# Transposes by a 32-column selection matrix, and an expansion moved ahead of two stores, in a gated mix of attention and memory recurrence

## The chip, the cores and the metric

The kernel runs on one core of a Trainium2 chip. TensorE (PE) does the matrix products out of SBUF into PSUM, VectorE (DVE) and ScalarE (ACT) read PSUM and SBUF, GpSimd (POOL) works on SBUF alone, and SyncE (SP) and POOL issue the DMAs. Each engine takes its instructions in order, so an instruction that waits holds all that stand behind it on its engine. The metric is the device time of one execution in microseconds. Before the change its median is 6508.05 us, over 6 runs from 6499.43 to 6512.82.

## What is computed

Forward and backward of a gated mix of two branches over 2048 tokens of width 576. Branch A is attention with 32 query heads of 18 and one shared key and value head. Branch B is a recurrence over 64 segments of 32 tokens: 8 memory rows `mem` stand in front of the segment's tokens, attention with 32 heads of 128 runs over the 40 rows, and the memory's output rows are the next segment's memory.

```python
g = sigmoid((x * gate_w).sum(-1, keepdims=True))
a = A(x, A_wq, A_wk, A_wv, A_wo)
...
for s in range(n_seg):
    h = concatenate([mem, xs])
    q, k, v = h @ Wq, h @ Wk, h @ Wv        # 32 heads of 128
    p = softmax(where(mask, q @ k.T * scale, -1e9))
    o = (p @ v) @ Wo
    mem = o[:8]
    outs.append(o[8:])
return g * a + (1 - g) * b                   # and its gradients for 11 inputs
```

The loop over segments can't be run in parallel: segment s needs the memory that segment s − 1 leaves.

## The kernel before

**Two weaves.** `weave` (L211) runs two generators against each other. After each piece of the chain (up to its `yield`) it runs one step of the sweep. Within a weave the instructions stand on each engine in just this order; no scheduler moves them. In the forward weave (L1707) the chain is `b_chain_fwd`, which is the recurrence of B for the memory rows, and the sweep is `a_pass1`, the attention of A. In the backward weave (L1715) the chain is `b_chain_bwd` and the sweep is `a_pass2`.

**The sweep's step** is the same each time: two score products `a_S` (32 rows deep, 512 wide), two products `a_dP`, the exponential `a_E` of the scores on ACT (L1394), two products `a_W` on DVE (L1424) that read a_dP and a_E, and eight accumulation products `a_acc`. `a_S` has one buffer, so the scores of a step wait until the exponential of the step before has read it. `a_dP` has two, so each waits for the `a_W` that reads the step before. The backward sweep is built alike, with names b_S, b_dP, b_E (L1532), b_dS (L1553), b_acc. I call a piece of the chain with the step that follows it a slot. A segment has 16 pieces and a block of A's sweep has 16 steps, so the same pieces always meet: `a_post` (L1453) puts its transposes into the slots of k's and q's transposes, and its chain of small POOL operations, which ends with the product `a_qt` (L1494), in front of POOL's work on v.

**A segment of the forward chain.** The 8 memory rows (with 24 token rows that ride along) lie transposed in `hm`. For w in k, q, v two products of 512 columns by `proj` give row tiles `c_k2`, `c_q2`, `c_v2` of 128 partitions × 8 × 128 (the profile calls them c_k, c_q, c_v): partition 32c + r holds row r of head group c, and only r below 8 are memory rows. `mem_T` (L231) transposes such a tile: eight 128x128 transposes (L71) into one PSUM bank in bf16, of whose 128 columns per block 32 are read, the 8 memory rows of each of 4 groups. ACT copies k's and v's into `mT` (L308), and DVE copies q's into `c_qT` (L334). The row tiles go to DRAM by `rows_out` (L298, POOL's queue), and from there by `rows_copy` (L303 and L305, SP's queue) into the token tables. Then come scores, their exponential `c_E`, the denominators, and the probabilities `c_pn` (L366, DVE). `expand` (L205, POOL) spreads them over block diagonals `c_PB`. The pieces from v's second half on are these:

- v's second projection; the load of the next keys `c_kx` (SP); the store of v's rows `vrow_dram`; `c_pn`; its store `pm_dram` (L367); `c_PB`
- `rows_copy("q")` on SP; `mem_T` of v; its copy and store
- 16 products of `c_vx` and `c_v2` with `c_PB` into a tile `c_x`; DVE copies it to `c_oT` (L381)
- four pieces with the output projection (`half`, tile `c_pj`, copied by ACT to `c_hs`) and the sums that give the next segment's `hm`

**Backward.** In `b_chain_bwd` `mem_T` is called once per segment, on `dOm` (L856), and ACT copies the result to `r_dOT` (L858). `seln` (L136) is a constant selection matrix in bf16, 128 × (4 × 8), with a one where row 32c + q meets column (c, q). The backward chain already multiplies other row tiles by it (`r_x<-seln,r_dx`).

Of the kernel before, what the change touches and what calls it, by code (L numbers as in the profile page):

```python
# [9 lines left out]
BF16 = mybir.dt.bfloat16  # L10
F32 = mybir.dt.float32
P = 128
# [18 lines left out]
class Kern:  # L31
# [197 lines left out]
        return pj  # L229

    def mem_T(self, t2, psum, tag, bufs):  # L231
        pt = psum.tile([P, 8, P], BF16, name=tag, bufs=bufs)
        for u in range(8):
            self.tr(pt[:, u, :], t2[:, u, :], P)
        return pt[:].rearrange("p u (c t) -> p u c t", t=32)[:, :, :, 0:8]

    def b_chain_fwd(self, keep, sp, psum):
        nc = self.nc
# [21 lines left out]
        def load_k(s):  # L260
            kx = sp.tile([P, HB, 32], BF16, name="c_kx", bufs=1)
            nc.sync.dma_start_transpose(kx[:], self.xtok["k"][s * 32:(s + 1) * 32, :])
            return kx
# [23 lines left out]
        for s in range(NSEG):  # L287
            h_ = hm[s % 2]
            nc.gpsimd.dma_start(self.memT_dram[:, :, s, :], h_[:, :, 0:8])
            t2 = {w: sp.tile([P, 8, E], BF16, name=f"c_{w}2", bufs=1) for w in ("k", "q", "v")}  # L290
# [6 lines left out]
            def rows_out(w):  # L297
                nc.gpsimd.dma_start(self.row_dram[w][s], t2[w][:].rearrange("p u e -> p (u e)"))  # L298

            def rows_copy(w):  # L300
                src = self.row_dram[w][s].rearrange("(c r) e -> c r e", r=32)
                t0, n = ride(s)
                nc.sync.dma_start(self.mtok[w][s * 8:(s + 1) * 8, :].rearrange("r (c e) -> c r e", c=4), src[:, 0:8, :])  # L303
                if n:
                    nc.sync.dma_start(self.xtok[w][t0:t0 + n, :].rearrange("r (c e) -> c r e", c=4), src[:, 8:8 + n, :])  # L305
# [42 lines left out]
            for u in range(8):  # L348
                for c in range(4):
                    self.mm(ps[32 * c:32 * c + 8, 64 + 8 * u:72 + 8 * u], lhsT=mT["k"][:, c, u, :],  # L350
                            rhs=qT[:, u, c, :], start=False, stop=True, tp=(0, 32 * c))
# [9 lines left out]
            proj("v", 1)  # L361
            if s + 1 < NSEG:
                kx = load_k(s + 1)
            rows_out("v")
            pn = sp.tile([P, 2, 64], BF16, name="c_pn", bufs=1)
            nc.vector.tensor_tensor(out=pn[:], in0=Et[:], in1=rd[:].unsqueeze(1).to_broadcast([P, 2, 64]), op=ALU.mult)  # L366
            nc.gpsimd.dma_start(self.pm_dram[s], pn[:].rearrange("p a b -> p (a b)"))  # L367
            PB = sp.tile([P, 16, 4, 8], BF16, name="c_PB", bufs=1)
            self.expand(PB[:], pn[:].rearrange("p a (u q) -> p (a u) q", q=8), 16)
            yield  # L370
            rows_copy("q")
            src = self.mem_T(t2["v"], psum, "c_pj", 1)
# [1426 lines left out]
```

## Time and profile before

| | us |
|---|---|
| median of 6 runs | 6508.05 |
| the profiled execution, its own time | 6504.03 |
| its span, first to last instruction | 6501.8 |
| forward weave, about | 497 to 2470 |
| backward weave, about | 3285 to 5070 |

| in the trace | count | ns of one |
|---|---|---|
| transposes c_x<-identB,c_k and c_q; c_pj<-identB,c_v; r_x<-identB,r_dOm | 512 each | 219 |
| products c_x<-c_PB,c_vx; r_x<-seln,r_dx | 512 each | 176 |
| c_PB, POOL | 64 | 1084 |
| issue of vrow_dram, POOL | 64 | 607 |
| issue of pm_dram, POOL | 64 | 538 |
| c_qT from PSUM in bf16, DVE | 64 | 292 |
| c_oT from PSUM in F32, DVE | 64 | 425 |

A row of the timeline gives the start in us, the length in us, the engine, the line, the operation with output<-inputs, shapes and count, and in brackets how long the engine had been idle before it and what ended that. PEld is the loading of weights, which runs beside PE. Matmuls overlap: 8 of 219 ns take 0.61 us together. A wait's row gives the waiting operation and what it waited for, the total in us, how often, and the longest.

### The profile page before, as it was taken

The page shows a single profiled execution, that of the slowest core. Times are in us where ns is not written, and L with a number is a line of the kernel's source. Part 1 is how long each engine was busy: PE and PEld are TensorE (multiplying, and loading weights), DVE is VectorE, ACT ScalarE, POOL GpSimd, SP SyncE. Part 2 cuts the span into 40 slices and gives each one's busy share as a digit, 9 for nine tenths or more (in the row PEclk, how much of TensorE's full clock was granted, in tenths as well). Part 3 has the DMA queues.
Part 4 walks back from the last instruction along what each step waited for, and adds up shares of the span by engine and source line. Part 5 has one row for each costly group of instructions (what it writes and reads, how often), then busy time and mean ns, then how long its engine had stood idle before and what let it go on. Part 6 is the DMA issues. An engine that isn't in the chain of part 4 may idle for free. (4 is left out here: it accounts for less than half of the span.)

```text
span 6501.8 us, 208836 instructions
## 1 busy us (share of the span) xinstructions
PE 5984.0 (92%) x88822; PEld 3370.7 (52%) x88822; DVE 3770.0 (58%) x7061; ACT 3493.2 (54%) x5105; POOL 1960.4 (30%) x3451
## 2 busy tenths in 40 slices
PE   7898999999999995999969999999999899899997
PEld 5443444444444443877734444444444677675443
DVE  4336777777777773666658888888888211111111
ACT  3326777777777773666547777777777322211101
POOL 3002333333333333444423333333333111112212
PEclk9999999999999997999989999999999999999998
DMA  4636666666665445999864444443444899896643
GB/s 151 224 145 113 117 116 118 119 115 118 116 117 103 96 83 144 251 260 258 247 204 101 100 99 101 103 102 100 101 102 102 202 239 242 226 280 206 219 151 111
DMA packets 1368109, 991.95 MB, mean 153 GB/s; under 512 B 931613, under 2 KB 1184806, under 8 KB 1356486
## 3 DMA queue, kind: packets, MB, share of 16 engines
q1 hardware_dynamic: 1285030, 780.53, 50.5%
q0 software_dynamic: 82144, 198.05, 9.8%
q8 instruction: 696, 11.40, 0.8%
q14 instruction: 239, 1.96, 0.1%
HBM read 552.41 MB, written 384.76 MB: 144 GB/s over the span
## 5 line engine op out<-in xcount | busy, mean ns | idle before, releaser
L1424 DVE TENSOR_TENSOR a_W<-a_dP,a_E 128x512 bf16<-128x512 f32 x2048 | 1314.7, 684 | 472.0 <-PE a_dP L66 437.2
L1553 DVE TENSOR_TENSOR b_dS<-b_dP,b_E 128x512 bf16<-128x512 f32 x2048 | 1315.2, 684 | 322.1 <-PE b_dP L66 239.3
L1532 ACT ACTIVATE b_E<-b_S 128x1024 bf16<-128x1024 f32 x1024 | 1048.9, 1024 | 505.0 <-PE b_dP L66 355.6
L1394 ACT ACTIVATE a_E<-a_S 128x1024 bf16<-128x1024 f32 x1024 | 1050.9, 1026 | 170.1 <-PE a_dP L66 157.6
L66 PE MATMUL b_dP<-b_KV,b_QD 32*128 32x512 bf16 x2048 | 594.8, 380 | 5.5 <-DVE b_dS L1553 5.3
L66 PE MATMUL b_S<-b_KV,b_QD 32*128 32x512 bf16 x2048 | 399.2, 383 | 103.9 <-ACT b_E L1532 50.3
L66 PE MATMUL a_dP<-a_QD,l_KV 32*128 32x512 bf16 x2048 | 489.5, 382 | 0.8 <-DVE a_W L1424 0.4
L66 PE MATMUL w_acc<-w_d,w_h 128*128 128x512 bf16 (+1 forms) x2400 | 473.8, 379 | 0.0
L66 PE MATMUL r_pj<-WT,r_dT 128*32 128x288 bf16 x12288 | 443.8, 286 | 0.0
L66 PE MATMUL a_S<-a_QD,l_KV 32*128 32x512 bf16 x2048 | 399.0, 384 | 45.6 <-ACT a_E L1394 42.7
L66 PE MATMUL a_acc<-a_W,l_WK 128*32 128x512 bf16 x4096 | 410.3, 390 | 0.1
L66 PE MATMUL b_acc<-b_dS,b_SD 128*32 128x512 bf16 x2048 | 403.8, 390 | 0.0
L66 PE MATMUL b_acc<-b_E,b_SD 128*32 128x512 bf16 x2048 | 403.3, 390 | 0.0
L66 PE MATMUL a_acc<-a_E,l_VK 128*32 128x512 bf16 x4096 | 399.4, 380 | 0.0
L66 PEld LDWEIGHTS <-r_dT 128*32 128x32 bf16 x12288 | 329.3, 97 | 77.4 <-issue 0.6
L1027 DVE COPY y_T<-y_pt 128x512 bf16<-128x512 bf16 x256 | 97.0, 419 | 469.4 <-PE y_pt L71 451.1
L66 PEld LDWEIGHTS <-w_h 128*128 128x128 bf16 (+1 forms) x2400 | 213.0, 100 | 244.6 <-issue 3.4
L66 PEld LDWEIGHTS <-b_SD 128*32 128x32 bf16 x4096 | 105.2, 92 | 431.4 <-issue 430.4
L66 PEld LDWEIGHTS <-hm 128*32 128x32 bf16 x7680 | 206.4, 97 | 230.2 <-issue 15.5
L66 PEld LDWEIGHTS <-b_QD 32*128 32x128 bf16 x4096 | 140.5, 91 | 306.8 <-issue 213.9
L1013 ACT CAST y_tdk<-y_pk 128x512 bf16<-128x512 f32 x128 | 75.1, 587 | 381.1 <-PE y_pk L66 226.0
L66 PEld LDWEIGHTS <-l_WK 128*32 128x32 bf16 x4096 | 105.3, 93 | 325.1 <-issue 325.0
(412 smaller groups left out, 11714.2 us busy)
## 6 DMA issues: line engine op xcount, KB each, us to landing
b_QD<-qd_dram SPq DMA_DIRECT2D x256, 128.0 KB
b_SD<-sd_dram SPq DMA_DIRECT2D x256, 128.0 KB
dOx_dram<-p_tok SPq DMA_DIRECT2D x16, 1024.0 KB
c_vx<-vx_dram SPq DMA_DIRECT2D x256, 64.0 KB
krow_dram<-c_k POOLq DMA_DIRECT2D x64, 256.0 KB, 2.8
qrow_dram<-c_q POOLq DMA_DIRECT2D x64, 256.0 KB, 2.6
vrow_dram<-c_v POOLq DMA_DIRECT2D x64, 256.0 KB, 3.2
x_q<-qx_dram SPq DMA_DIRECT2D x32, 512.0 KB
```

The costliest lines, as they stand in the source:

```text
L66: return self.nc.tensor.matmul(out, lhsT, rhs, start=start, stop=stop, tile_position=tp, skip_group_check=True)
L1013: nc.scalar.copy(d[w][:, r, :], pk[:])
L1027: nc.vector.tensor_copy(T_[t][w][:], pt[:])
L1394: nc.scalar.activation(E_[n][:], S.pop(n)[:], ACT.Exp, scale=SCALEA)
L1424: nc.vector.tensor_tensor(out=W_[n][:, i, :], in0=dP[i][:], in1=E_[n][:, i, :], op=ALU.mult)
L1532: nc.scalar.activation(E_[n][:], S.pop(n)[:], ACT.Exp, scale=SCALEA)
L1553: nc.vector.tensor_tensor(out=D_[n][:, i, :], in0=dP[i][:], in1=E_[n][:, i, :], op=ALU.mult)
```

## The change

`mem_T` no longer transposes whole blocks. Each of its 8 matmuls keeps the row block as weights, but the moving matrix is `seln` with 32 columns instead of the identity with 128, so that only the 32 memory columns are produced. They are ordinary products now and leave F32 in PSUM, in a tile of 1 KB per partition where 2 KB stood. In the forward chain `c_pn` and `expand` come first in their piece, then the store of `pm_dram`, then that of v's rows. On POOL the order vrow_dram, pm_dram, c_PB becomes c_PB, pm_dram, vrow_dram; the other engines' order stays.

```diff
     def mem_T(self, t2, psum, tag, bufs):
-        pt = psum.tile([P, 8, P], BF16, name=tag, bufs=bufs)
+        pt = psum.tile([P, 8, 32], F32, name=tag, bufs=bufs)
         for u in range(8):
-            self.tr(pt[:, u, :], t2[:, u, :], P)
-        return pt[:].rearrange("p u (c t) -> p u c t", t=32)[:, :, :, 0:8]
+            self.mm(pt[:, u, :], lhsT=t2[:, u, :], rhs=self.seln[:].rearrange("p c q -> p (c q)"))
+        return pt[:].rearrange("p u (c t) -> p u c t", t=8)
...
             if s + 1 < NSEG:
                 kx = load_k(s + 1)
-            rows_out("v")
             pn = sp.tile([P, 2, 64], BF16, name="c_pn", bufs=1)
             nc.vector.tensor_tensor(out=pn[:], in0=Et[:], in1=rd[:].unsqueeze(1).to_broadcast([P, 2, 64]), op=ALU.mult)
-            nc.gpsimd.dma_start(self.pm_dram[s], pn[:].rearrange("p a b -> p (a b)"))
             PB = sp.tile([P, 16, 4, 8], BF16, name="c_PB", bufs=1)
             self.expand(PB[:], pn[:].rearrange("p a (u q) -> p (a u) q", q=8), 16)
+            nc.gpsimd.dma_start(self.pm_dram[s], pn[:].rearrange("p a b -> p (a b)"))
+            rows_out("v")
             yield
```

## The prediction

> **What bounds the kernel now.** I read the page's busy rows first, then the windows, to find the stages that hold the change.
>
> ```profile
> span 6501.8 us, 208836 instructions
> PE 5984.0 (92%) x88822; PEld 3370.7 (52%) x88822; DVE 3770.0 (58%) x7061; ACT 3493.2 (54%) x5105; POOL 1960.4 (30%) x3451
> ```
> ```profile
> 900.00:1200.00 300.00, 288.73 (x5278) 136.79 (x5275) 220.86 (x394) 220.87 (x306) 104.65 (x212) 1.00 0.64 117
> 3900.00:4200.00 300.00, 287.88 (x5481) 142.25 (x5474) 247.73 (x440) 212.88 (x264) 100.44 (x176) 1.00 0.42 102
> ```
>
> The second fence's columns are window, length, busy PE, PEld, DVE, ACT, POOL, granted clock, DMA share and GB/s. In both weave stages PE is busy 96% at clock 1.00. That isn't proof that PE sets every slot, because PE's busy time counts latency: a queue of short waits hides in it. So next I took PE's waits in the forward weave (497 to 2470 us).
>
> ```profile
> PE a_S L66 <- ACT a_E L1394: 42.7, 189, 1.1
> PE c_x L66 <- POOL c_PB L205: 32.6, 62, 1.4
> ```
>
> Two waits count: the sweep's next scores waiting for the exponential (189 times), and the chain's output products waiting for POOL's expanded block (62 times, 0.53 us each). The timeline of one segment shows where they stand:
>
> ```profile
> 1203.36 0.62 PE L71 MATMUL c_pj<-identB,c_v 128*128 128x128 bf16 x8
> 1203.49 0.61 POOL L298 DMA_DIRECT2D vrow_dram<-c_v  x1
> ...
> 1204.10 0.54 POOL L367 DMA_DIRECT2D pm_dram<-c_pn  x1
> 1204.17 0.39 PE L66 MATMUL a_S<-a_QD,l_KV 32*128 32x512 bf16 x2 [0.19 <-ACT a_E L1394]
> ...
> 1204.65 1.08 POOL L205 TENSOR_TENSOR c_PB<-c_pn,bmask 128x512 bf16<-128x512 bf16 x1
> ...
> 1204.70 1.29 DVE L1424 TENSOR_TENSOR a_W<-a_dP,a_E 128x512 bf16<-128x512 f32 x2 [0.39 <-PE a_dP L66]
> ...
> 1205.79 0.18 PE L66 MATMUL c_x<-c_PB,c_vx 128*128 128x32 bf16 x1 [0.51 <-POOL c_PB L205]
> ```
>
> POOL finishes a_pass1's block a_qt at 1203.41 (1202.31 + 1.10), then issues two stores (0.61 + 0.54 with gaps), and only then expands. PE stands 0.51 us.
>
> **Part 1, the expansion ahead of the stores.** Per segment it moves one POOL operation of 1.08 us past two POOL DMA issues; nothing is added. c_pn is ready at 1202.03 + 0.47 = 1202.50, before POOL is free, so the new order's wait on DVE costs nothing. c_PB runs about 1203.42 to 1204.50. PE can use it from 1205.28 (the accumulation matmuls start at 1204.89, the weights load at 1205.21, and 1205.79 − 0.51 = 1205.28). Cover 0.8 us: the 0.51 goes whole. What is late next?
> - a_S: its exponential (ACT, 1204.65 + 1.02) ends 1205.67, and the 16 products with their tail took 1206.27 − 1205.79 = 0.48 us, so scores start at about 1205.76 instead of 1206.27.
> - The second a_dP needs the buffer that a_W frees at 1204.70 + 1.29 = 1205.99. In this trace the second a_dP starts about 0.05 us after such a release, so 1206.04 instead of 1206.28. The accumulation behind it gains only **0.24 us**.
> - c_oT on DVE no longer waits for PE: 1205.99 instead of 1206.39, so the next a_W starts at about 1206.42 instead of 1206.81 and ends at 1207.71. Before, it ended 1206.81 + 1.29 = 1208.10 and held the next second a_dP by 0.1 us (that slot's a_dP row is 0.49 long instead of 0.39). This hold goes too: 0.24 + 0.11 = **0.35 us** is kept at the next accumulation. The output projection needs c_oT at about 1206.8 and has it at 1206.42.
>
> From there to the next segment the slots are mostly PE's, so the whole loop moves up by 0.35 us. 62 × 0.35 = **21.7 us**. Ends: 0.24 × 62 = 15 and 0.51 × 62 = 32; I take 0.35, worked out from the neighbouring slots.
>
> What goes later: pm_dram's issue by 0.4 us, vrow_dram's by 1.62 (1.08 + 0.54), c_vmT's store not at all (it follows all three in both orders). On SP, L303 copies vrow; behind it stand the weight stash and the next segment's ride load. The store lands 3.2 us (median) after its issue, at worst 6.3: 1205.11 + 3.2 = 1208.3. SP comes to that copy at 1211.52, 0.35 earlier in future: cover 2.9 us. Free.
>
> **Part 2, the 32-column products.** mem_T is called for k, q and v forward and dOm backward: 4 × 64 = 256 calls of 8 matmuls. Before, a call's row is 0.61 for 8 with 0.219 each: (0.61 − 0.219)/7 = 56 ns apart. The new form, 128x128 weights with 32 moving columns, stands in the trace as c_x<-c_PB,c_vx and r_x<-seln,r_dx: 176 ns long, 25 ns apart (1205.79, .81, .84). That is 8 × 31 = **0.25 us** less PE per call, 63 us in all if PE alone set each slot.
>
> Here a rule speaks against the change. The Trainium skill, "TensorE: Matmul & The Clock Gate", section LDWEIGHTS, prices a weight load by its columns: 128/1.2 = 107 ns, and its table of weight-path modes gives fast loading as about twice that speed, an estimated 53 ns. Both forms load the same 128x128 weights, so by the rule fewer moving columns would save at most 56 − 53 = 3 ns each, 6 us in all. The row of 25 ns, each matmul with a fresh weight load, decides: 63 us at most.
>
> But the slots decide what is kept:
>
> ```profile
> 1218.36 1.29 DVE L1424 TENSOR_TENSOR a_W<-a_dP,a_E 128x512 bf16<-128x512 f32 x2 [0.67 <-PE a_dP L66]
> ...
> 1219.19 0.61 PE L71 MATMUL c_x<-identB,c_k 128*128 128x128 bf16 x8
> ...
> 1219.74 0.39 PE L66 MATMUL a_dP<-a_QD,l_KV 32*128 32x512 bf16 x2
> ```
> ```profile
> 1224.24 1.03 ACT L1394 ACTIVATE a_E<-a_S 128x1024 bf16<-128x1024 f32 x1
> ...
> 1225.32 0.39 PE L66 MATMUL a_S<-a_QD,l_KV 32*128 32x512 bf16 x2
> ...
> 1225.39 0.29 DVE L334 COPY c_qT<-c_x 128x256 bf16<-128x256 bf16 x1
> ```
>
> - **k**: a_W ends 1219.65, so the second a_dP cannot start before 1219.70, against 1219.75 now. 0.04–0.05 us × 64 = 2.6 us.
> - **q**: the exponential ends 1225.27 and a_S starts 1225.32. Already ACT's: 0.
> - **v**: 1203.09 + 1.03 = 1204.12, a_S at 1204.17 after a wait of 0.19, which becomes 0.44: 0.
> - **dOm**: backward, b_E runs 4024.58 to 4025.60 and b_S starts 4025.66: 0. dOT's copy moves up 0.1 us, but the slots behind it again start on b_E.
>
> The results are now F32 in PSUM. ACT's copies don't change (r_dOT from bf16 373 ns, r_dT from F32 366). DVE's c_qT does: 292 ns from bf16, against 425 for c_oT, also 256 elements, from F32: +0.13 us × 64 = 8.5 us. It is hidden: DVE idles 0.17 us between c_qT and the next a_W, which waits for a_dP. Without that cover it would cost up to 8.5 us.
>
> **Sum.** 21.7 + 2.6 = 24 us. Profiled execution: span 6501.8 → 6478, its own time 6504.0 → 6480. That run is 4.0 below the median 6508.05, so the median goes to **6484**.
>
> **Rivals.**
> - *A: the shorter transposes pay more.* For it: k's slot is 1.9 us long with a_S 0.28 us behind the exponential's end, so a_S itself can move. Against: the second a_dP, and the ACT-bound slots of q, v, dOm. If k pays in full: 0.25 × 64 = 16 + 21.7 = 38, 6470. All four in full: 63 + 21.7 = 85, 6423; I give that almost nothing. Chance 0.14.
> - *B: the gain is handed to the next wait.* c_oT or a_W holds the following slot, a later ACT-bound slot absorbs the lead, or c_qT's 8.5 us shows. Gain 0 to 15, about 6500. For it: 189 waits on the exponential. Against: these slots start from PE's previous scores, so they shift along. Chance 0.21.
> - *C: slower, SP falls behind.* If vrow_dram lands after SP reaches L303 (1211.17 in the new order), SP's queue and with it the rides and k rows of later segments are late. It decides from a landing of 6.1 us after the issue; at 6.5 it eats the 24 us (0.39 × 62). If SP had no cover at all: 1.62 × 62 = 100 − 24 = +76, 6584. Against: median landing 3.2, and SP waits for POOL's a_t and the stash's stores each segment, which absorbs lateness. Chance 0.10.
> - *That it doesn't do what it says*: the orders of POOL and PE show both edits in the program; only their worth is open.
>
> **Numbers.** Main case 0.55, its own range 6476 to 6493. 0.2% of 6508 is 13 us, what such a measurement can tell from no change: the border is 6495. Main and A are faster (0.69), B partly (0.06), so faster 0.75, same 0.15, slower 0.10. The range 6464 to 6504 takes in k's full gain, the 32 us end and most of B.
>
> **What would show it.** Right: PE's wait on c_PB gone; a_S's wait on a_E longer (v's slot 0.44); c_k, c_q, c_v products 25 ns apart and 176 long; c_qT about 425; segment length down about 0.38 us; backward stage unchanged. Wrong: a backward stage that shortens (A), the slots after c_oT no shorter than before (B), PE waiting for hm, c_kx or c_vx (C).

## The result, and the profile after

The changed kernel takes **6489.44 us**, the median of 20 runs (6478.34 to 6504.5). 40 runs of the kernel before, on the same chip, have a median of 6504.77. The ratio is 0.9979 with a 95% interval of 0.9973 to 0.9985: 13.7 us less (9.8 to 17.6). The forecast was 24 us less. The profiled execution's own time is 6484.8, against 6504.03 before.

The page's first rows, after:

```profile
span 6483.0 us, 208775 instructions
PE 5938.8 (92%) x88822; PEld 3330.0 (51%) x88822; DVE 3768.4 (58%) x7061; ACT 3480.1 (54%) x5105; POOL 1955.5 (30%) x3451
```

PE's busy time fell by 45.2 us and the span by 18.8. Busy time that isn't on the path doesn't shorten the span, so the waits come next. PE's waits in the forward weave, 497 to 2470 us:

```profile
PE a_S L66 <- ACT a_E L1394: 72.0, 245, 1.1
...
PE c_x L66 <- issue: 3.0, 3, 1.9
PE c_pj L66 <- issue: 3.0, 1, 3.0
PE c_pj L66 <- ACT c_hs L422: 2.7, 3, 1.8
```

The row of c_x waiting for c_PB (32.6 us, 62 times) is gone. The scores' wait for the exponential has grown from 42.7 to 72.0. At the bottom stand small rows, among them one single stop of 3.0 us put down to "issue": I come back to them.

The timeline around v's slot, after:

```profile
1201.45 0.37 PE L66 MATMUL c_pj<-seln,c_v 128*128 128x32 bf16 x8
1201.45 1.06 POOL L205 TENSOR_TENSOR c_PB<-c_pn,bmask 128x512 bf16<-128x512 bf16 x1
...
1202.26 0.39 PE L66 MATMUL a_S<-a_QD,l_KV 32*128 32x512 bf16 x2 [0.44 <-ACT a_E L1394]
...
1202.46 0.61 POOL L368 DMA_DIRECT2D pm_dram<-c_pn  x1
...
1203.08 0.54 POOL L298 DMA_DIRECT2D vrow_dram<-c_v  x1
...
1203.30 0.19 PE L66 MATMUL c_x<-c_PB,c_vx 128*128 128x32 bf16 x1
```

c_PB ends at 1202.51, 0.8 us before the products that read it, and both stores have moved behind it. The wait of a_S is 0.44 as forecast: what the transposes gave back, the exponential took.

To see what a segment gained I read the start of every score product of the sweep from the trace. From one to the next is a slot; there are 64 segments of 16 slots. For each of the 16 positions I took the median over the segments:

| us | slots of c_PB and the two behind | slot of k's transposes and the next | all 16 |
|---|---|---|---|
| before | 6.244 | 3.858 | 30.436 |
| after | 5.884 | 3.804 | 30.022 |
| difference | 0.360 | 0.054 | 0.414 |
| forecast | 0.35 | 0.04 | 0.38 |

64 × 0.414 = **26.5 us** is the regular gain. But the first score to the last one took 1953.3 us before and 1939.0 after, only 14.2 less. The rest lies in slots far off their usual length. I added up what all slots are longer than the median of their position, where that is over 0.3 us: 6.0 us before, 18.4 after. I call this sum the **stray time**. (The expectations below call it stalls, and count some 1.7 us more in every kernel.) It took back 12.4 of the 26.5 us. What the span fell beyond the weave's 14.2 us lies outside of these slots.

One of the stray places, in the timeline after, in the pieces of the output projection:

```profile
782.05 0.40 PE L66 MATMUL c_pj<-WoN,c_oT 128*32 128x64 bf16 x30
782.60 0.62 SPq L295 DMA_DIRECT2D oh_dram<-c_oh  x1
785.41 0.24 PE L66 MATMUL c_pj<-WoN,c_oT 128*32 128x64 bf16 x2 [2.95 <-issue]
...
786.63 0.17 DVE L419 CAST hm<-c_x 128x16 bf16<-128x16 f32 x1 [3.52 <-PE c_x L66]
786.69 0.21 ACT L422 COPY c_hs<-c_pj 128x64 f32<-128x64 f32 x1 [3.94 <-PE c_x L66]
```

PE stops in the middle of a row of products with the same operands, two before its end. The profile shows nothing that another engine owes it, and DVE and ACT then wait for PE. The windows before, in and behind this stop (window, length, busy PE, PEld, DVE, ACT, POOL, granted clock, DMA share, GB/s):

```profile
776.00:782.20 6.20, 6.18 (x149) 3.66 (x144) 4.42 (x9) 3.78 (x6) 2.03 (x5) 1.00 0.64 77
782.30:785.40 3.10, 0.15 (x22) 0.05 (x6) 0.81 (x2) 0.44 (x1) 0.00 (x0) 0.99 0.94 245
785.50:792.10 6.60, 6.60 (x52) 2.54 (x51) 2.81 (x6) 2.26 (x3) 1.60 (x2) 0.50 0.62 70
```

In the stop the DMA engines are busy at 0.94 and PE at 0.05. Then the granted clock is 0.50 for 6.6 us, with PE never idle: the stop is paid for a second time. In this profile there are two more such pairs in the weave: PE idle for 1.79 us from 625.0 and for 1.88 us from 1299.8, each followed by a stretch at half clock. At 625.0 the profile puts PE's wait down to ACT's c_hs, but ACT and DVE stood too, with their operands complete by its records. The profile of before shows no half-clock stretch between 540 and 2430 us.

What was PE waiting for? The DMA view of 782 to 787 us lists the queues by packets, MB and share:

```profile
q1 hardware_dynamic: 3902, 0.61, 68.8%
q0 software_dynamic: 144, 0.39, 21.5%
q8 instruction: 1, 0.02, 1.2%
```

One packet of a queue named "instruction" is among them. Its record starts at 783.11 and takes 0.95 us; PE goes on 1.35 us after it lands. At 1296.85 such a packet took 3.38 us and PE went on 1.49 us after it; at 624.04, 0.96 us, and PE's next product came 1.82 us after. The 14 profiles of this study hold 22 stops of PE over 1 us in the forward weave, apart from those at its first scores and those that wait for c_PB. 21 of them end 1.0 to 2.5 us after such a packet has landed, the other 2.54; any moment of the weave has a chance of about 0.26 of that. In the weave there are 267 packets of 16 KB, 4.37 MB, which is about 64 bytes for each of the 68,025 matmuls and weight loads that PE runs there. So I take the stops for PE's own program coming in late. That is an inference from times and sizes; no run tests it by itself.

### The profile page after: what moved, and what is told of

Same layout as the page of the kernel before. It is cut to its first block, busy times and chain, and to the rows that moved or that the text cites. A ratio compares the mean times of both kernels' runs of the same rounds, so it can differ in the third digit from the quotient of the medians.

```text
span 6483.0 us, 208775 instructions
## 1 busy us (share of the span) xinstructions
PE 5938.8 (92%) x88822; PEld 3330.0 (51%) x88822; DVE 3768.4 (58%) x7061; ACT 3480.1 (54%) x5105; POOL 1955.5 (30%) x3451
## 5 line engine op out<-in xcount | busy, mean ns | idle before, releaser
L66 PE MATMUL a_dP<-a_QD,l_KV 32*128 32x512 bf16 x2048 | 513.2, 383 | 1.0 <-DVE a_W L1424 0.8
```

Source lines behind the costliest of these rows:

```text
L66: return self.nc.tensor.matmul(out, lhsT, rhs, start=start, stop=stop, tile_position=tp, skip_group_check=True)
```

## The experiments

What the change moves on POOL, beside c_PB, is the store of v's rows, 256 KB per segment. Its row in the tile view, before and after, minimum, median and maximum from issue to landing:

```profile
DMA to landing us min/median/max: 3.0/3.2/6.3
```
```profile
DMA to landing us min/median/max: 3.7/5.1/5.8
```

The trace tells the landing of only 8 of the 64 stores in each of the two.

The question is which part brings the 26.5 us of regular gain and what loses 12 of them. Diffs are against the changed kernel where nothing else is said.

**Each part alone.** e1_expand_first has the transposes of before and the new order:

```diff
-        pt = psum.tile([P, 8, 32], F32, name=tag, bufs=bufs)
+        pt = psum.tile([P, 8, P], BF16, name=tag, bufs=bufs)
...
-            self.mm(pt[:, u, :], lhsT=t2[:, u, :], rhs=self.seln[:].rearrange("p c q -> p (c q)"))
+            self.tr(pt[:, u, :], t2[:, u, :], P)
```

> The change's second part alone: c_PB before pm_dram and vrow_dram, transposes as before. Theory T1 (per-slot gain as forecast, then irregular stalls of 2 to 3 us with all engines still, which grow because the moved store of v's rows now falls in with the copies of q's rows and the c_vx load): wait on c_PB gone, slots 10 to 12 together 0.36 us shorter in the median, sum of slots far over their median well above the 8 us of before, time about -11 us. T2 (the missing time belongs to the products, part 2): no more stalls than before, time -20 to -23 us. T3 (stalls of the profiles are chance; the slots themselves gain less on average): -10 us with slot medians that gain less than 0.36.

e2_products_only has the new products and the order of before:

```diff
+            rows_out("v")
             pn = sp.tile([P, 2, 64], BF16, name="c_pn", bufs=1)
...
+            nc.gpsimd.dma_start(self.pm_dram[s], pn[:].rearrange("p a b -> p (a b)"))
             PB = sp.tile([P, 16, 4, 8], BF16, name="c_PB", bufs=1)
...
-            nc.gpsimd.dma_start(self.pm_dram[s], pn[:].rearrange("p a b -> p (a b)"))
-            rows_out("v")
```

> The change's first part alone: 32-column products, POOL's order as before. Forecast of the prediction: -2.6 us (k's slot and the next together 0.05 us shorter, q, v and the backward stage unchanged), within what can't be told from no change. T2 (products cost time elsewhere): slower by some 5 to 10 us. Rival A of the prediction (the transposes pay more): -10 us or better. c_qT 414 to 425 ns instead of 292.

Measured: e1 0.9976 (0.9966 to 0.9986), 15.6 us less (one of its ten runs, of 13216 us, is left out); e2 1.0005 (0.9997 to 1.0014), no change that can be told. The waits of PE in e2's forward weave show both of the old rows in new sizes:

```profile
PE a_S L66 <- ACT a_E L1394: 73.4, 252, 1.1
PE c_x L66 <- POOL c_PB L205: 32.4, 61, 1.4
```

The wait for c_PB is there in full, and the wait for the exponential is as long as in the changed kernel. So the 30 us by which that wait grew come from the shorter products: PE is done sooner and waits longer. The regular gain is 3.4 us for e2 and 23.0 for e1. The order carries nearly all of it, and with it comes the stray time: 20.3 us in e1, 6.7 in e2. Yet e2 too measures 6.6 us less than its regular gain (the table below), with the store in its old place. Its profiled weave shows only 0.9 of that, so this part stays unexplained.

**Another place or queue for v's store.** e3_vrow_last puts it on POOL behind everything of the segment's output product; e4_vrow_on_sp gives it to SP, right behind v's second projection and ahead of the load of c_kx.

```diff
-            rows_out("v")
             yield
...
             nc.gpsimd.tensor_copy(oh[:], oT[:].rearrange("p u c q -> p c u q"))
+            rows_out("v")
```

> The changed kernel with the store of v's rows still later on POOL, behind c_oh. T1: the store's place decides, so the time differs from the changed kernel's ratio 0.9979: if the burst with the q row copies and the c_vx load is what hurts, the store leaves its first half but joins the c_vx load; stalls of the same size or fewer, -14 to -24 us. If SP's copy of v's rows now waits for the landing (SP's copy of vrow starts later or lasts longer), rival C of the prediction: the gain shrinks to 0 or turns. T3: -14 us, as the changed kernel.

```diff
             proj("v", 1)
+            nc.sync.dma_start(self.row_dram["v"][s], t2["v"][:].rearrange("p u e -> p (u e)"))
             if s + 1 < NSEG:
...
-            rows_out("v")
```

> The changed kernel with the store of v's rows issued by SP ahead of the c_kx load instead of by POOL, so about 1 us earlier and on the other DMA queue; POOL only issues pm_dram behind c_PB. T1: fewer stalls than in the changed kernel if its lateness is the cause, -20 to -25 us. T3: -14 us. Against both: SP's own queue gets 0.6 us longer per segment and the c_kx load starts later; if SP has no room, slower than the changed kernel.

Measured: e3 0.9969 (0.9958 to 0.998), 20 us less, stray time 8.7; e4 **0.9952** (0.994 to 0.9964), 31 us less, stray time 2.3. In e3 SP's copy of v's rows waits for the store 51 times between 600 and 2400 us, 134 us in all, and the kernel is none the slower for it: SP has the room that rival C doubted (in the changed kernel it waits there twice, 3.3 us). The timeline of e4 around v's slot:

```profile
1191.73 1.07 POOL L205 TENSOR_TENSOR c_PB<-c_pn,bmask 128x512 bf16<-128x512 bf16 x1
...
1192.69 0.39 SPq L362 DMA_DIRECT2D vrow_dram<-c_v  x1
1192.74 0.61 POOL L369 DMA_DIRECT2D pm_dram<-c_pn  x1
...
1193.18 1.37 SPq L262 DMA_TRANSPOSE c_kx<-kx_dram  x1
...
1193.58 0.19 PE L66 MATMUL c_x<-c_PB,c_vx 128*128 128x32 bf16 x1
```

c_PB ends at 1192.80, the products begin at 1193.58: POOL gives PE no more than in the changed kernel, and the regular gain is the same (26.4 us). Yet the whole of it reaches the time. The loss thus isn't a part of c_PB's going first. It goes with how the store is issued.

**How early, and on which queue.** Four more places and one load moved away. e5_vrow_before_pm: on POOL, the order c_PB, vrow_dram, pm_dram.

```diff
-            nc.gpsimd.dma_start(self.pm_dram[s], pn[:].rearrange("p a b -> p (a b)"))
             rows_out("v")
+            nc.gpsimd.dma_start(self.pm_dram[s], pn[:].rearrange("p a b -> p (a b)"))
```

> The changed kernel with the two stores behind c_PB swapped: vrow_dram, then pm_dram, so v's rows start 0.55 us earlier than in the changed kernel and 1.1 us later than before the change. If the lateness of this store is what makes the stalls (place theory), stalls between those of before (8 us) and of the changed kernel (20 us), -17 to -22 us. If what helped in the run with the store on SP was the queue and not the time (queue theory), -13 us as the changed kernel. Slot medians as in the changed kernel, 30.02 us per segment.

e6_vrow_on_sp_late: on SP as in e4, but behind the load of c_kx.

```diff
                 kx = load_k(s + 1)
+            nc.sync.dma_start(self.row_dram["v"][s], t2["v"][:].rearrange("p u e -> p (u e)"))
...
-            rows_out("v")
```

> The store of v's rows on SP behind the c_kx load, so about as late as POOL issues it in the changed kernel. Place theory: the stalls come back, -13 to -18 us. Queue theory: they stay away, -28 to -32 us as with the store on SP ahead of the load.

e7_vx_load_later: the changed kernel with the load of the next c_vx two pieces later, so that it and the store don't run together.

```diff
             if s + 1 < NSEG:
-                vx = load_v(s + 1)
...
                         nc.scalar.copy(hs[:, 0:hi - lo], ph[:, 0:hi - lo])
+                    if lo == 512:
+                        vx = load_v(s + 1)
```

> The changed kernel with the c_vx load of the next segment issued two pieces later (behind the third part of the output projection), so that it no longer falls in with the store of v's rows and the copies of q's rows. If the stalls are late instruction packets in a burst of these transfers (burst theory), fewer stalls than the 20 us of the changed kernel, -18 to -26 us, and no long PE stop that ends 1.3 to 1.8 us after an instruction packet lands in slots 11 to 13. If the stalls have to do with POOL's queue alone, -13 us, stalls as before.

e8_before_sp_store: the kernel *before*, with nothing but the store given to SP.

```diff
             proj("v", 1)
+            nc.sync.dma_start(self.row_dram["v"][s], t2["v"][:].rearrange("p u e -> p (u e)"))
             if s + 1 < NSEG:
                 kx = load_k(s + 1)
-            rows_out("v")
```

> The kernel before, both parts undone, with nothing changed but the store of v's rows issued by SP instead of POOL. POOL reaches c_PB 0.6 us earlier, so the wait of 0.53 us on it should go without any reordering: slots 10 to 12 together 0.36 us shorter, as with c_PB first, k's slots unchanged (30.08 us per segment). If the reordering itself is worth nothing beyond POOL's time ahead of c_PB, and SP's queue keeps the stalls away: -27 to -30 us. If the old order with SP's store has stalls: -12 to -20 us.

Measured: e5 0.9963 (0.995 to 0.9976); e6 0.9960 (0.9947 to 0.9972); e7 0.9982 (0.9973 to 0.999); e8 0.9961 (0.9949 to 0.9974). The first row of PE's waits in e8's forward weave:

```profile
PE a_S L66 <- ACT a_E L1394: 44.4, 194, 1.1
```

It is the row of the kernel before, whose second row, c_PB's, is gone in e8 as well. Taking one issue of 0.61 us off POOL is enough; the expansion need not pass pm_dram's store. e7 was to free the store from the c_vx load, and its loss stays: that the two run together is not the cause. The landings agree with no simple rule, as far as the few known ones go: a median of 3.7 us in e7 (8 of 64), and in e3, which lost less, 5.6 (16 of 64). e6 issues its store 2.4 us behind the first of v's products, later than the changed kernel (1.6), and keeps its gain. e5 issues it on POOL 0.6 us earlier than the changed kernel and loses 2.2 us. So neither the lateness alone nor POOL's queue alone explains the loss.

**Other transfers, and a repeat.** e9_q_copies_later moves q's copies from row table to token table one piece later; e11_kx_load_later moves the load of c_kx from v's piece into the output projection.

```diff
             yield
-            rows_copy("q")
             src = self.mem_T(t2["v"], psum, "c_pj", 1)
...
                 head_out()
+                rows_copy("q")
                 rows_copy("v")
```

> The changed kernel (store of v's rows on POOL behind pm_dram) with the copies of q's rows issued one piece later on SP, behind the c_vx load. If these copies are what the late store meets, the stalls shrink from 20 us to 10 or less and the time to -20 to -28 us. If not, -12 to -16 us as the changed kernel, stalls of 15 us or more.

```diff
             proj("v", 1)
-            if s + 1 < NSEG:
-                kx = load_k(s + 1)
...
+                kx = load_k(s + 1)
                 head_out()
```

> The changed kernel with the transposing load of the next segment's keys c_kx moved behind the c_vx load, two pieces later. If this load is the partner of the late store: stalls 10 us or less, -20 to -28 us. If not: stalls of 15 us or more, -12 to -16 us.

e12_sp_store_no_products is e4 with the transposes of before (the two changes shown at e1 and e4), and e10_sp_store_again is e4 unchanged.

> The best kernel so far (c_PB first, v's rows stored by SP ahead of the c_kx load) with the transposes as before the change. What the products are worth where stalls are few: by the prediction 2.6 us, by the slot medians of the runs 3.5 us, so 3 us slower than the same kernel with products, -27 to -29 us. If the products cost time (the +3 us measured for them alone): faster than with products, -33 us or better.

> The changed kernel with v's rows stored by SP, once more, to be compared with the run without the products on the same chip: -29 to -33 us, stalls of 3 to 8 us. If the narrow band of the first time was chance, times between -20 and -31.

Measured: e9 0.9975 (0.9966 to 0.9985); e11 0.9969 (0.9958 to 0.9981); e12 0.9961 (0.9947 to 0.9975); e10 0.9957 (0.9944 to 0.9969). e12 gains 2.6 us less than e10. That is the size of the products' regular 3.4 us, though within the noise, and it gives no sign that the products cost time, as e2 alone might suggest.

All kernels beside each other. The regular gain is 64 times the difference of the slot medians; the measured gain is one minus the ratio, times the median of before in the same session (6493 to 6505 us).

| | v's store | regular gain | measured gain | measured − regular | stray time |
|---|---|---|---|---|---|
| after | POOL, behind c_PB, pm_dram | 26.5 | 13.7 | −12.8 | 18.4 |
| e1 | same | 23.0 | 15.6 | −7.4 | 20.3 |
| e7 | same | 26.3 | 11.7 | −14.6 | 17.2 |
| e9 | same | 26.5 | 16.3 | −10.2 | 13.8 |
| e11 | same | 26.6 | 20.2 | −6.4 | 8.8 |
| e3 | POOL, later still | 26.5 | 20.1 | −6.4 | 8.7 |
| e5 | POOL, 0.6 us earlier | 26.3 | 24.1 | −2.2 | 13.3 |
| e2 | POOL, ahead, as before | 3.4 | −3.2 | −6.6 | 6.7 |
| e4 | SP, ahead of c_kx | 26.4 | 31.2 | +4.8 | 2.3 |
| e10 | SP, ahead of c_kx | 26.5 | 28.0 | +1.5 | 10.1 |
| e12 | SP, ahead of c_kx | 23.0 | 25.4 | +2.4 | 6.9 |
| e8 | SP, ahead of c_kx | 22.8 | 25.4 | +2.6 | 6.3 |
| e6 | SP, behind c_kx | 26.3 | 26.0 | −0.3 | 8.4 |

A measured gain is uncertain by 4 us for the changed kernel and by 5 to 9 for the others, and the stray time is that of one execution (e4 and its repeat: 2.3 and 10.1), so single rows prove little. The groups do: with the store on SP the five kernels keep their regular gain, 2.2 us above it on average. With the store on POOL directly behind the other two, the five lose 10.3 us on average, and their stray time is 15.7 against 6.8. e3, later still on POOL, loses 6.4. That split was seen on after and e4 first; e6, e8, e10 and e12 were run afterwards and fell on the same side as e4.

**What stays open.** What exactly holds PE up, and how the store has a part in it. Neither the c_vx load (e7) nor q's copies (e9) is the partner alone. The c_kx load is the nearest: e11's 20.2 us less is at the edge of what was expected if it were (20 to 28), though the interval (12 to 27 us) decides nothing. The traces say more. SP issues the c_kx load 0.85 us behind the store in the kernel before, and 0.65 us ahead of it in the changed one (medians). After the store's issue its first 4 KB packet starts as follows, beside what the forward weave of the same execution gained less than its regular gain:

| | issue to first packet, median (longest), us | missing in the weave, us |
|---|---|---|
| before | 1.33 (2.17) | |
| e2 | 1.32 (1.94) | 0.9 |
| after | 2.82 (6.04) | 12.3 |
| e1 | 2.32 (5.00) | 12.7 |
| e7 | 2.57 (5.87) | 9.9 |
| e9 | 1.83 (5.35) | 5.7 |
| e11 | 1.29 (3.15) | 1.0 |
| e5 | 1.29 (3.78) | 6.4 |

The longest delay, 6.04 us, is that of the segment with the stop at 782: the store is issued at 776.01, and its packets run at the start of the stop. The segment of the stop at 625.0 has 4.83, but that of 1299.8 only 1.13. So a store issued right behind the c_kx load is held up, and where it is held up more, more is lost, roughly and with e5 excepted. Moving that load away (e11) takes both back. This is an order among single executions, not a test, and how a held-up store reaches PE isn't shown by it. A run of e11 often enough to settle its time is missing, and so is a trace that tells which of the 16 DMA engines a packet used.

**The best version** is e4: 6461.04 us (6459.3 to 6462.8) against 6493.39, and 6474.4 against 6502.91 in the repeat. It beats the changed kernel by about a quarter of a per cent and the one before by 0.4 to 0.5%.

## Why the prediction was right in its direction and too large

- **The wait on c_PB, right.** The kept 0.35 us were worked out from the neighbouring slots; they are 0.36, in all 64 segments where the sum took 62. The two ends of 0.24 and 0.51 are both excluded.
- **The transposes, right.** The timeline of k's slot, after:

```profile
1216.09 1.29 DVE L1424 TENSOR_TENSOR a_W<-a_dP,a_E 128x512 bf16<-128x512 f32 x2 [0.66 <-PE a_dP L66]
...
1216.92 0.35 PE L66 MATMUL c_x<-seln,c_k 128*128 128x32 bf16 x8
...
1217.23 0.39 PE L66 MATMUL a_S<-a_QD,l_KV 32*128 32x512 bf16 x2
1217.24 0.56 PE L66 MATMUL a_dP<-a_QD,l_KV 32*128 32x512 bf16 x2
...
1217.73 0.40 PE L66 MATMUL a_acc<-a_W,l_WK 128*32 128x512 bf16 x4
```

  a_W ends at 1217.38. The pair of a_dP is 0.56 long, where two free ones take 0.39: the second stands behind a_W. The scores come 0.225 us sooner than before, and the next slot gives all but 0.054 back. The eight products take 0.35, so they are (0.35 − 0.176)/7 = 25 ns apart, where the rule (the Trainium skill, "TensorE: Matmul & The Clock Gate", section LDWEIGHTS, with its table of weight-path modes) gave an estimate of 53: the row was rightly preferred. The rule prices one load, and here the loads overlap: in v's slot each takes 0.10 us and all eight 0.27. Of 0.25 us saved per call, k keeps 0.054 and q and v none.
- **c_qT, right.** Its row in the tile view, median in ns in the middle (292 before, 425 forecast), hidden as forecast:

```profile
L334 DVE CAST c_qT<-c_x x64: 411/414/426, 521.1 to 2431.9; 128x256 bf16<-128x256 f32 x64
```

- **Backward, right.** From the first score b_S to the last it is 1781.8 us before and 1781.2 after. So close an agreement is chance (the other profiles lie between 1775.2 and 1787.5), but no shortening shows. PE's first wait row there, before and after, is the saving of dOm's products handed to the exponential:

```profile
PE b_S L66 <- ACT b_E L1532: 49.1, 202, 0.4
```
```profile
PE b_S L66 <- ACT b_E L1532: 82.9, 322, 0.6
```

- **The step that failed** is this one: "What goes later: … vrow_dram's by 1.62 … cover 2.9 us. Free." The cover was reckoned for the copy on SP that reads the store, and there it all but held: in the changed kernel that copy waits for the store twice between 600 and 2400 us, 3.3 us in all, PE's waits for hm are 18.1 us against 19.8 before, and for c_vx 0.5 against 0.2. (The landing of 3.2 us that it took rests on the 8 stores of 64 whose landing the trace tells.) But the sum put at nothing what a later store costs anything else. With the store on SP, where the same regular gain arises, the kernels gain 25 to 31 us, as the forecast's 24 said; with the store on POOL directly behind the other two, 10.3 us of it are lost on average, 12.8 in the changed kernel. The traces show this loss as stops of PE and stretches at half clock, and a store whose packets start 2.8 us after its issue instead of 1.3; by what path the one leads to the other stays open. The other terms together were 2.5 us too small (26.5 against 24).
- **The rivals.** A (the transposes pay more) is excluded by k's slot and the backward stage. B had the size (its 0 to 15 us hold the 13.7) but not the mechanism: no regular slot gave back the gain. C put the loss on SP's queue; the loss is real but half of what would have made the kernel slower, and not on SP.
- **Luck.** The prediction drew the border to "same" at 13 us. The 13.7 measured are hardly past it, and their interval (9.8 to 17.6) lies on both sides: that the kernel came out on the faster side of this border isn't settled by the runs.

## What to carry to other kernels

Where DMA issues stand ahead of work on the critical path, try giving one to another queue before pushing them all back on the same one: here the first alone brought 25 us, and the second, with shorter products besides, 14. When a transfer is moved, its cover at the reader is only a part of its price: here a store issued 1.5 us later on POOL cost some 10 us that no reader's wait shows. Look at what is issued just ahead of its new place, and at when its packets start. A gain that shows in every segment's median but not in the total is to be sought in the few slots far off their median.

## What the runs showed of the hardware

- PE stood for 1.1 to 2.95 us 22 times in the 14 forward weaves, at 782 in the middle of a row of like products with nothing owed to it that the profile shows. 21 of the 22 stops ended 1.0 to 2.5 us after the landing of a packet of the instruction queue. That these packets are PE's program is inferred.
- After three such stops the granted clock was 0.50 for 3.4 us (behind 1299.8) or about 6.8 us (behind 625.0 and 782.5), although the stops were only 1.79 to 2.95 us long. Such a stop costs its own length, and then the slots at half clock are longer too. Not every one is followed so: a stop of 1.10 us at 2032.7 in the kernel before was not.
- Products of 128x128 weights with 32 moving columns stood 25 ns apart, each with a fresh weight load of 0.10 us; with 128 columns, 56 ns.
- The packets of a 256 KB store on POOL's queue started 1.3 us after the issue where it stood ahead of SP's transposing load c_kx, and 2.8 us (up to 6.0) where it stood 0.65 us behind it.
